# Second MLP product as Strassen's seven half products, queries and keys in a ring of three head groups, output projection's weights fetched per unit

## The chip, the cores and the metric

One core of one Trainium2 chip. The metric is device microseconds of one execution, from the first instruction to the last. The kernel before was run three times: 1659.76, 1660.66 and 1661.33 us, median 1660.66 us.

## The reference, cut to what matters

```python
def A(x, wqkv, wo):                      # x: 2048 x 640, 32 heads of 20
    q, k, v = split(x @ wqkv)            # 640 x 1920
    scores = einsum("hqd,hkd->hqk", q, k) * 20 ** -0.5
    p = softmax(where(0 <= query - key < 256, scores, -1e9))
    return merge_heads(einsum("hqk,hkd->hqd", p, v)) @ wo      # 640 x 640
def B(x, w1, b1, w2, b2):                # w1: 640 x 1536, w2: 1536 x 640
    return relu(x @ w1 + b1) ** 2 @ w2 + b2
for layer in range(2):                   # the same weights in both layers
    x = x + A(layernorm(x), wqkv, wo)
    x = x + B(layernorm(x), w1, b1, w2, b2)
```

Inputs and output are float32.

## The kernel before

**Precision.** Every float32 operand of a dense product is kept as two float16 parts, a high part and the rest, its low part. `mm3` (L256) forms a product as three chains of TensorE matmuls, high by high, high by low and low by high, accumulated in one PSUM tile. Whatever feeds a matmul therefore has two evictions: ScalarE writes the high part, then VectorE the low part (`hh` for the hidden layer at L823 and L826, `qd` for queries and keys at L411 and L414, `od` for the attention output at L733 and L736, `yl` for the layer norm at L348 and L352).

**Units and quads.** The work is cut into 16 units: two layers, each of eight blocks of 256 rows. Since a query sees 256 keys back, a unit needs the keys of its own block and of the block before. The 32 heads are handled as 8 quads of four heads, two quads to a head group. For each quad `max_quad` multiplies queries by keys to find the largest score of each row (matmuls at L523, masked maxima on VectorE at L535), `max_out` transposes the maxima and writes them as two more rows under the queries (L547 to L560), `exp_quad` multiplies again with those rows included and takes the exponential on ScalarE (L585, L598; GpSimd masks at L613 and L617), and `pv_quad` multiplies by the values (L647), copies the result (L659, `ot`) and writes it to DRAM (L664, `o<-ot`). `max_quad` runs three quads ahead of `exp_quad`.

**Through DRAM and back.** Queries and keys are computed for a unit by `stage_qk`, evicted as `qd` (L411, L414), written to DRAM by L445 and L447 (`qk<-qd`) and read back by L451 into `qt` and `kt`, laid out with the head dimension on the partitions. `kt` holds all heads of one block, three of them in turn. The attention output of a unit is read back in `load_o` once all its quads are written: `rs` (L693, the sums of the exponentials, spread over partitions) and `od` (L694). VectorE and ScalarE then make it ready for the output projection in an **od chain** of four pieces on VectorE: reciprocal of `rs` (L726), product (L729), and the low part (L736), with ScalarE's high part (L733) between the last two.

**Layer norm to matmul.** `layernorm` (L273 to L286) leaves its rows with tokens on the partitions. For a unit's queries, keys and values, `ln_cross` (L368 to L371, using `cross`, L335 to L361) makes the high (L348) and low (L352) parts of its two row blocks in `yl`, and four DMA transposes, one for each part of each block (L355), turn them into `yT`. The matmuls of `stage_qk` read `yT`.

**What runs beside what.** In the main loop, unit u carries three kinds of work at once: the quads of unit u (`exp_quad`, `pv_quad`), the `max_quad`s three ahead, and a chain of dense work of other units, sliced in between by `together`. In the steady units the dense chain is, in this order: `stage_qk(u+1)` for the queries, `stage_v(u+1)` (first half), `stage_o(u-1)`, `y_cross(u-1)`, `stage_qk(u+1)` for the keys, the rest of `stage_v`, and `stage_f(u-1)`, which holds the first MLP product (f1, weights `w1`, 180 matmuls of 256 columns), relu on ScalarE (L816), the square on GpSimd (L820), the two evictions into `hh`, a call of `ln_cross(u+2)`, and then the second MLP product (f2): 144 matmuls `acc<-w_s,hh` of 320 columns in four banks, each added to `x` on VectorE (L853) and stored (L862). `load_o(u-1)` is called after the first half quad of unit u. I call the place where f2 of one unit ends and `stage_qk` of the next begins the **unit boundary**.

**What sets the order.** The program is written by a planner that runs while the kernel is built. Each eviction or DMA is a `Job` with an engine, a cost, what it depends on and a priority; `pump` puts out the jobs that it thinks can start, `need` moves its clock to a job's end. What it puts out becomes the order of each engine's queue, and on the chip each engine takes its queue strictly in that order, whenever its turn really comes. All DMAs are issued by SyncE, one queue. There are two PSUM banks for dense tiles, transposes and value products (`mm_tile`), so the matmul after next needs the eviction of the tile two before, and three pairs of banks for scores.

## Time and profile before

| what | before |
|---|---|
| runs | 1659.76, 1660.66, 1661.33 us, median 1660.66 us |
| the profiled execution: its span | 1660.5 us |
| TensorE busy, share of the span | 1595.4 us, 96% |
| VectorE, ScalarE, GpSimd busy | 1032.8, 750.1, 636.8 us |
| TensorE busy between 332 and 1411 us, the steady units | 1077.03 us of 1079.00 |
| moved by DMA | 157.42 MB, mean 95 GB/s |

How to read it: the span of the profiled execution is the time of that one run. The page's first part gives how long each engine was busy, its second part the same in 40 slices of 41.5 us, its fourth the chain of work that ended last. The answers of the trace show groups of instructions as `line engine operation output<-input (partitions x elements, type) xcount`, with the busy time, the mean of one in ns, and the idle time of the engine just before them with its releaser; the timeline shows `start duration engine ...`, in us, with the wait in square brackets; and the windows show, for each stretch, its length and then busy us and count for PE, PEld, DVE, ACT and POOL, the granted TensorE clock, the mean DMA share and GB/s.

### The profile page before, as it was taken

How to read it: one execution, taken by the hardware profiler on the slowest of the kernel's cores; microseconds unless marked ns; L12 is line 12 of the kernel's file. 1: busy time of each engine (PE TensorE's matmuls, PEld its weight loads, DVE VectorE, ACT ScalarE, POOL GpSimd, SP SyncE). 2: the span in 40 equal slices, each digit the busy share in tenths (PEclk: the TensorE clock that was granted, in tenths of full speed). 3: DMA queues.
4: the chain of work that ended last, by engine and by line, in shares of the span. 5: the costliest groups of instructions: out<-in, count | busy, mean ns of one | idle time of the engine just before them, and what ended most of it. 6: DMA issues, size and time to landing. Idle time of an engine off the chain costs nothing.

```text
span 1660.5 us, 44547 instructions
## 1 busy us (share of the span) xinstructions
PE 1595.4 (96%) x17574; PEld 1173.0 (71%) x17574; DVE 1032.8 (62%) x3231; ACT 750.1 (45%) x1616; POOL 636.8 (38%) x1309
## 2 busy tenths in 40 slices
PE   7787899999999999999999999999999999999989
PEld 5564676777777777777777777777777777776667
DVE  7566657675665766566565756657665666757341
ACT  4455534535444454544434354444545444453512
POOL 1343533524344353424414243443534344353512
PEclk9897999999999999999999999999999999999999
DMA  8465214343452534335153433424343352421020
GB/s 245 129 179 155 61 61 107 63 118 84 100 101 60 125 69 113 78 102 118 50 136 74 123 82 104 98 68 118 73 109 80 104 115 50 108 70 53 26 64 17
DMA packets 231484, 157.42 MB, mean 95 GB/s; under 512 B 79468, under 2 KB 215020, under 8 KB 231276
## 3 DMA queue, kind: packets, MB, share of 16 engines
q1 hardware_dynamic: 231276, 154.59, 37.8%
q8 instruction: 138, 2.26, 0.6%
q14 instruction: 70, 0.57, 0.1%
HBM read 84.68 MB, written 52.95 MB: 83 GB/s over the span
## 4 chain that ended last, share of the span: by engine, by line
PE 87%; DVE 5%; ACT 3%; DMA 3%; issue 1%; SPq 1%; POOL 0%; DVEq 0%; ACTq 0%; POOLq 0%
PE acc L256 65%; PE pv L647 10%; PE bb L585 6%; PE bb L523 5%; DVE bb L535 2%; ACT pt L598 2%; DMA qk<-qd 1%; PE tr L547 1%; DMA qk<-yl 0%; DMA w_s<-in_A_wqkv_dram 0%; DVE mx L535 0%; DMA ov<-o 0%; DMA qt<-qk 0%; ACT r L816 0%; SPq L560 0%
## 5 line engine op out<-in xcount | busy, mean ns | idle before, releaser
L535 DVE CUSTOM_DVE_ANT_0 bb<-bb,maskb 128x384 f32<-128x384 f32 (+2 forms) x1024 | 510.4, 565 | 117.3 <-PE bb L523 109.4
L598 ACT ACTIVATE pt<-bb 128x512 f32<-128x512 f32 (+1 forms) x736 | 376.5, 602 | 239.9 <-PE bb L585 239.6
L613 POOL TENSOR_SCALAR_AFFINE_SELECT pt<-pt 128x256 f32<-128x256 f32 x448 | 195.0, 440 | 542.8 <-ACT pt L598 521.4
L256 PE MATMUL acc<-y,w_s 128*128 128x256 f16 x2880 | 331.8, 273 | 4.2 <-DVE y L304 1.4
L256 PE MATMUL acc<-w_s,hh 128*128 128x320 f16 x2304 | 326.2, 299 | 0.0
L256 PEld LDWEIGHTS <-w_s 128*128 128x128 f16 x2880 | 278.5, 98 | 58.2 <-issue 25.7
L256 PE MATMUL acc<-yT,wq_s 128*128 128x256 f16 x2400 | 282.7, 276 | 12.6 <-DVE qd L414 10.6
L256 PEld LDWEIGHTS <-hh 128*128 128x128 f16 x2304 | 221.8, 98 | 97.8 <-issue 15.3
L256 PEld LDWEIGHTS <-wq_s 128*128 128x128 f16 x2400 | 233.7, 99 | 58.0 <-issue 27.8
L617 POOL TENSOR_SCALAR_AFFINE_SELECT pt<-pt 128x256 f32<-128x256 f32 x512 | 217.1, 446 | 64.3 <-ACT pt L598 63.2
L826 DVE TENSOR_TENSOR hh<-r,hh 128x256 f16<-128x256 f32 x192 | 91.7, 499 | 208.4 <-ACT hh L823 200.9
L647 PE MATMUL pv<-pt,vt 128*32 128x128 f32 (+1 forms) x3840 | 188.8, 331 | 2.0 <-POOL pt L617 1.4
L820 POOL TENSOR_TENSOR r<-r 128x256 f32<-128x256 f32 x192 | 113.5, 612 | 184.9 <-ACT r L816 183.4
L659 ACT COPY ot<-pv 128x256 f32<-128x256 f32 x128 | 47.6, 372 | 285.6 <-PE pv L647 285.6
L535 DVE DVE_READ_ACCUMULATOR2_ANT mx<- 128x1 f32 x1024 | 142.7, 139 | 0.1
L256 PE MATMUL acc<-wq_s,yT 128*128 128x320 f16 x960 | 142.0, 301 | 0.1
L647 PEld LDWEIGHTS pv<-pt,vt 128*32 128x32 f32 x3840 | 104.2, 110 | 49.1 <-issue 17.6
L256 PE MATMUL acc<-wo_s,od 128*128 128x320 f16 x900 | 131.9, 301 | 3.6 <-DVE x L758 1.7
L816 ACT ACTIVATE r<-acc,b1s 128x256 f32<-128x256 f32 x192 | 80.6, 471 | 99.8 <-PE acc L256 98.4
L256 PEld LDWEIGHTS <-yT 128*128 128x128 f16 x960 | 93.0, 98 | 40.4 <-issue 7.0
L585 PE MATMUL bb<-qt,kt 62*128 62x128 f16 (+1 forms) x1920 | 109.4, 246 | 10.6 <-DVE mx L535 9.8
L256 PEld LDWEIGHTS <-od 128*128 128x128 f16 x900 | 86.1, 98 | 45.9 <-issue 11.1
(84 smaller groups left out, 1175.7 us busy)
## 6 DMA issues: line engine op xcount, KB each, us to landing
qt<-qk SPq DMA_DIRECT2D x30, 480.0 KB
kt<-qk SPq DMA_DIRECT2D x30, 480.0 KB
qk<-qd SPq DMA_DIRECT2D x17, 640.0 KB
o<-ot SPq DMA_DIRECT2D x256, 42.0 KB
od<-o SPq DMA_DIRECT2D x13, 640.0 KB
qk<-yl SPq DMA_DIRECT2D x13, 640.0 KB
qk<-qd SPq DMA_DIRECT2D x17, 320.0 KB
xt<-in_A_x_dram SPq DMA_DIRECT2D x16, 320.0 KB
```

The lines of the kernel that those rows point to most:

```text
L256: nc.tensor.matmul(acc, lhs(a, c), rhs(b, c), start=(k == 0), stop=(k == 3 * nk - 1))
L523: nc.tensor.matmul(to, qt[r, p, i * P:(i + 1) * P], kt[r, p, a:b], start=True, stop=True)
L535: nc.vector.tensor_tensor_reduce(out=v, in0=v, in1=mask, scale=1.0, scalar=-3.0e38, op0=ALU.add, op1=ALU.max, accum_out=accum)))
L585: nc.tensor.matmul(bb[e][:, k, o:o + w], kt[r, 2 * qd + j, ko:ko + P], qt[r, 2 * qd + j, q0 * P:q0 * P + w], start=True, stop=True)
L598: nc.scalar.activation(box["pt"][:, :o], bb[e][:, k, :o], AF.Exp, scale=SCALE / (QS * QS))
L613: nc.gpsimd.affine_select(out=m, in_=m, pattern=[[0, 2], [-1, P]], compare_op=ALU.is_gt, fill=0.0, base=0, channel_multiplier=1)
L617: nc.gpsimd.affine_select(out=m, in_=m, pattern=[[0, 2], [1, P]], compare_op=ALU.is_ge, fill=0.0, base=0, channel_multiplier=-1)
L647: nc.tensor.matmul(pv[32 * jj:32 * (jj + 1), q0 * P:(q0 + qn) * P], vf[:, c:c + 32], pj[:, j, :], start=(k == 0), stop=(k == len(steps) - ...
L659: nc.scalar.copy(ot[:, qd % 2], pv)
L816: nc.scalar.activation(box["r"], acc[:, f, :], AF.Relu, bias=b1s[:, f0 + f:f0 + f + 1], scale=1.0 / (YS * WS))
L820: nc.gpsimd.tensor_tensor(box["r"], box["r"], box["r"], op=ALU.mult)
L826: nc.vector.tensor_sub(hh[:, 1, f, :], box["r"], hh[:, 0, f, :])
```

## The change

Three things are changed, and a few follow from them.

**f2 in seven half products.** Of the unit's hidden layer (256 rows by 1536) and of w2 (1536 by 640), each is cut in two along both directions. Strassen's scheme forms the four half-size blocks of the result from seven products of sums and differences of blocks, in place of eight. The seven products have 18 matmuls each of 320 columns: 126 a unit in place of 144, 2016 in place of 2304 in all. Each has an accumulator of its own that is added to one or two halves of `x` (L957, 12 adds a unit in place of four). The sums on the hidden side are made for each pair of f tiles, 6 a unit: two relus on ScalarE (L881), two squares and one sum on GpSimd (L885, L892), two sums on VectorE (`mid`, `ends`, L895 and L898), and three high (L907) and three low parts (L910), of 256, 384 and 256 columns. The tiles `ho` and `hw` take the place of `hh`. On the weights' side, seven combinations of w2 are made once at the start for each of 6 k (30 sums on GpSimd, 42 conversions of 320 columns in place of 12 of 640); the sixth k is staged in `r` and `sm`, the tiles in which the first f1 evictions work, and the first relu waits for it.

**A ring of head groups.** `qt` and `kt` give way to three tiles `qg` of queries and three `kg` of keys, each for one head group, with the block before and the unit's own block side by side. Keys are written into one DRAM tile a layer (L473, 3 DMAs) and each group's 256 or 512 keys loaded again for each unit (L503, L508). A matmul of `max_quad` can then run over both blocks: 12 a quad in place of 18, 1504 in place of 2176 in all, over the same columns. The DMAs that load queries and keys go from 72 to 256, and those of the program from 937 to 1162.

**wo from DRAM.** The converted `wo` is written to DRAM once (`wod`) and fetched for each unit with two DMAs right after `rs` and `od` (L753), into the space of `hw`.

With these, `stage_v(u+1, (3,))` and `ln_cross(u+2)` stand between f1 and f2 as chain items of their own, and `add_b2` (GpSimd, L832) is posted with `y_cross`. The instructions of the engines change as follows: PE 29256 to 27336, VectorE 3233 to 3681, ScalarE 1618 to 1736, GpSimd 1311 to 1429 (in the program's own counting).

The core of the diff:

```diff
+    qgs = [sb.tile([P, 4, T], F16, name=f"qg{i}") for i in range(3)]
+    kgs = [sb.tile([P, 4, 2 * T], F16, name=f"kg{i}") for i in range(3)]
-    wo_s = sb.tile([P, 2, KC, D], F16, name="wo_s")
+    wo_s = sb.tile([P, 2, KC, D], F16, name="wo", tag="hw", bufs=1)
+    wod = tc.dram_tile([P, 2, KC, D], F16, name="wod")
-    w2_s = sb.tile([P, 2, FC, D], F16, name="w2_s")
+    w2_s = sb.tile([P, FH, 2, 7, HD], F16, name="w2_s")
+    rt = sb.tile([P, 2, 5, P], F32, name="r")
+    sm = sb.tile([P, HD], F32, name="sm")
...
+        for j, fn, size in ((0, queries, 1.0), (1, keys, 1.6 if g else 1.0)):
+            deps = [w for c0, _, w in wrote[u, j] if c0 <= last]
+            job = dma(fn, int(8 * 3 * DH * T * 2 * size * (1.7 if u > 2 else 1.1)), *deps, n=2, prio=0)
...
+            wos[u] = wt, [dma(lambda wt=wt, a=a: nc.sync.dma_start(wt[:, a], wod[:, a]), P * 2 * KC * D, loaded, *keep,
+                              prio=1) for a in range(2)]
...
+    PRODS = ((1, "w", 2, "s", ((0, 0, 1.0), (0, 1, -1.0))), (4, "w", 3, "s", ((1, 0, -1.0), (1, 1, 1.0))),
+             (2, "o", 1, "o", ((1, 1, 1.0), (0, 1, 1.0))), (3, "w", 0, "d", ((1, 0, 1.0), (0, 0, 1.0))),
+             (0, "o", 2, "o", ((1, 0, 1.0), (0, 1, 1.0))), (5, "o", 0, "o", ((0, 1, 1.0),)),
+             (6, "w", 1, "d", ((1, 0, 1.0),)))
...
+        for t, to, c, k, dests in PRODS:
+            acc, jobs = mm_tile([P, 2 * T], "acc")
...
+            yield from mm3(acc[:, :HD], left, lambda b, f: w2_s[:, f, b, t], FH, 136, then)
...
-            parts += [stage_qk(u + 1, (0,)), stage_v(u + 1, range(2)), stage_o(u - 1), lambda: (y_cross(u - 1), iter(()))[1], stage_qk(u + 1, (1,)), stage_v(u + 1, range(2, 4))]
+            parts += [stage_qk(u + 1, (0,)), stage_v(u + 1, range(2)), stage_o(u - 1), lambda: (y_cross(u - 1), iter(()))[1], stage_qk(u + 1, (1,)), stage_v(u + 1, (2,))]
+            gap = [stage_v(u + 1, (3,))]
             if u + 2 < NU:
-                ahead_ln = u + 2
+                gap.append(lambda u=u: (ln_cross(u + 2, *b2js[u - 1]), iter(()))[1])
...
-        dense = chain(*parts, stage_f(u - 1, ahead_ln))
+        dense = chain(*parts, stage_f1(u - 1), *gap, stage_f2(u - 1))
```

Since the planner lays out the order anew, the queues differ around the unit boundary too. SyncE's queue at one steady unit boundary before: the four transposes of `yl` are the L355 rows, then come the last writes of the attention output (L664) and the loads of `rs` and `od`.

```order
L355 DMA_TRANSPOSE yT<-yl 128x5x128 x2
L862 DMA out_dram<-x_13582 128x640
L355 DMA_TRANSPOSE yT<-yl 128x5x128
L560 DMA qt<-mT 1x8x128 x4
L355 DMA_TRANSPOSE yT<-yl 128x5x128
L664 DMA o_13702<-ot 21x2x256 x4
L693 DMA rs<-o_13702 128x1x256
L694 DMA od<-o_13702 128x5x256
```

The same place after, where the lines are L383, L715, L742 and L743, and L753 is the fetch of `wo`:

```order
L383 DMA_TRANSPOSE yT<-yl 128x5x128 x3
L715 DMA o_15167<-ot 21x2x256 x4
L941 DMA out_dram<-x_15039 128x640
L742 DMA rs<-o_15167 128x1x256
L743 DMA od<-o_15167 128x5x256
L383 DMA_TRANSPOSE yT<-yl 128x5x128
L941 DMA out_dram<-x_15040 128x640
L762 DMA x_16555<-xs_121 128x640
L753 DMA wo<-wod 128x3200 x2
L762 DMA x_16556<-xs_122 128x640
```

The fourth transpose has moved behind the loads of `rs` and `od`, and the loads of `wo` and of `x` stand behind it.

VectorE's queue in the last quad before a steady unit boundary, before: the low parts of the layer norm's two blocks (L352, both at once) stand between one quad's maxima (L535) and an add of f2 (L853).

```order
L535 ISA bb,mx<-bb,maskb 128x3x128
L535 ISA mx 128x1
L853 SCALAR_TENSOR_TENSOR x_15120<-acc,x_15120 128x320
L352 TENSOR_TENSOR yl<-xt,yl 128x640 x2
L552 TENSOR_SCALAR mT<-tr 16x128
```

And after, where the maxima are L583, the low part of the layer norm's second block L380 and the last add of f2 L957:

```order
L583 ISA bb,mx<-bb,maskb 128x3x128
L583 ISA mx 128x1
L583 ISA bb,mx<-bb,maskb 128x3x128
L583 ISA mx 128x1
L380 TENSOR_TENSOR yl<-xt,yl 128x640
L957 SCALAR_TENSOR_TENSOR x_15040<-acc,x_15040 128x320
```

Before, both low parts have another eight maxima of the unit behind them; after, the second one has moved behind the unit's last eight maxima, one instruction ahead of f2's last add.

VectorE's queue across the boundary before, from the last maxima of the unit over the last add of f2 (L853) to the low part of the first two query columns (L414) and the start of the od chain (L726):

```order
L535 ISA bb,mx<-bb,maskb 128x3x128
L535 ISA mx 128x1
L535 ISA bb,mx<-bb,maskb 128x3x128
L535 ISA mx 128x1
L853 SCALAR_TENSOR_TENSOR x_15121<-acc,x_15121 128x320
L414 SCALAR_TENSOR_TENSOR qd<-acc,qd 128x2x256
L726 RECIPROCAL rs<-rs 128x64
```

And after, the twelve rows behind the last add of f2, where the od chain is L780, L783 and L790, and the low part of the query columns L438:

```order
L780 RECIPROCAL rs<-rs 128x64
L783 TENSOR_TENSOR od<-od,rs 128x5x64
L780 RECIPROCAL rs<-rs 128x64
L790 TENSOR_TENSOR od<-od 128x5x64
L783 TENSOR_TENSOR od<-od,rs 128x5x64
L780 RECIPROCAL rs<-rs 128x64
L790 TENSOR_TENSOR od<-od 128x5x64
L783 TENSOR_TENSOR od<-od,rs 128x5x64
L780 RECIPROCAL rs<-rs 128x64
L790 TENSOR_TENSOR od<-od 128x5x64
L783 TENSOR_TENSOR od<-od,rs 128x5x64
L438 SCALAR_TENSOR_TENSOR qd<-acc,qd 128x2x256
```

The query columns' low part has moved from ahead of the od chain to behind its fourth product. Of the twelve steady unit boundaries (those at which units 3 to 14 begin) eleven stand in this order on both engines; at the one where unit 8 begins, the first of the second layer, all four transposes stand ahead of the loads.

On TensorE the order at the boundary is, after: the last value product of the unit (L698, 16 matmuls), 24 matmuls of the last two half products, 16 of `exp_quad` (L634), and then `stage_qk` with 45 matmuls, 12 of `max_quad` (L571), the next value product (L698) and 30 more of `stage_qk`. Before, it is the same with 28 matmuls of f2, 16 of `exp_quad`, 50 of `stage_qk`, 18 of `max_quad` and the value product.

More of the change, by code (lines that the diff above doesn't have):

```diff
@@ L28 @@
 FC = F // P
+FH = FC // 2
 NP = H // 2
@@ new lines, in load_groups, with load_group, of, queries @@
+    def load_groups():
+        while ring["next"] < min(4 * NU, ring["free"] + 3):
+            u, G = divmod(ring["next"], 4)
+            last = (160 * (G + 1) - 1) // P
+            if any(wrote.get((u, j), [(0, 0, None)])[-1][1] <= last for j in range(2)):
+                return
+            load_group(u, G, last)
+            ring["next"] += 1
+    def load_group(u, G, last):
+        l, g = divmod(u, NG)
+        s, ps_ = (4 * u + G) % 3, slice(4 * G, 4 * G + 4)
+        def of(dr, e):
+            return dr.rearrange("(p e d) t n -> e (d t) p n", e=2, d=DH)[e][:, ps_]
+        def queries():
+            for e in range(2):
+                nc.sync.dma_start(qgs[s][64 * e:64 * e + 3 * DH], of(rows_of[u], e))
+        def keys():
+            lo = 0 if g else T
+            for e in range(2):
+                nc.sync.dma_start(kgs[s][64 * e:64 * e + 3 * DH, :, lo:],
+                                  of(kds[l], e)[:, :, (g - 1) * T + lo:(g + 1) * T])
+        for j, fn, size in ((0, queries, 1.0), (1, keys, 1.6 if g else 1.0)):
+            deps = [w for c0, _, w in wrote[u, j] if c0 <= last]
+            job = dma(fn, int(8 * 3 * DH * T * 2 * size * (1.7 if u > 2 else 1.1)), *deps, n=2, prio=0)
+            for q in range(2):
+                trips[u, j, 2 * G + q] = job
+        if u == 0 and G == 2:
+            job.gates.append(gate)
+        if u == 0 and G == 0:
+            job.gates.append(gate0)
```

372 lines of the change are left out of this document (209 added, 163 removed).

## The prediction

> **What bounds the kernel now.** I read the page first, then windows by stage, then the timeline over one unit boundary. The page's span, busy times, the rows of PE and PEclk over 40 slices, and the chain's shares by engine:
>
> ```profile
> span 1660.5 us, 44547 instructions
> PE 1595.4 (96%) x17574; PEld 1173.0 (71%) x17574; DVE 1032.8 (62%) x3231; ACT 750.1 (45%) x1616; POOL 636.8 (38%) x1309
> PE   7787899999999999999999999999999999999989
> PEclk9897999999999999999999999999999999999999
> PE 87%; DVE 5%; ACT 3%; DMA 3%; issue 1%; SPq 1%; POOL 0%; DVEq 0%; ACTq 0%; POOLq 0%
> ```
>
> The windows put the idle time of TensorE in its place (columns: stretch, length, busy of PE, PEld, DVE, ACT, POOL, clock, DMA share, GB/s):
>
> ```profile
> 0.00:332.00 332.00, 286.05 (x2973) 205.64 (x2974) 210.17 (x672) 163.49 (x337) 124.24 (x235) 0.94 0.47 125
> 332.00:1411.00 1079.00, 1077.03 (x12209) 799.67 (x12207) 699.65 (x2195) 489.87 (x1063) 422.45 (x892) 1.00 0.40 94
> 1411.00:1660.50 249.50, 232.30 (x2397) 167.70 (x2395) 122.95 (x365) 96.75 (x216) 90.08 (x182) 0.99 0.21 56
> ```
>
> For 1079 us TensorE is busy for 1077.03 at clock 1.00. Matmuls taken away there are gained in full, and any wait put in there is lost in full. What keeps the unit boundary closed shows in the timeline:
>
> ```profile
> 1005.29 1.55 DVE L352 TENSOR_TENSOR yl<-xt,yl 128x640 f16<-128x640 f32 x2
> 1010.25 1.21 SPq L355 DMA_TRANSPOSE yT<-yl  x1
> 1011.73 0.84 PE L523 MATMUL bb<-kt,qt 60*128 60x128 f16 x18
> 1012.49 1.51 PE L647 MATMUL pv<-pt,vt 128*32 128x256 f32 x32
> 1013.93 3.98 PE L256 MATMUL acc<-w_s,hh 128*128 128x320 f16 x28
> 1014.49 1.36 SPq L664 DMA_DIRECT2D o<-ot  x4
> 1017.19 0.59 SPq L693 DMA_DIRECT2D rs<-o  x1
> 1017.84 0.83 PE L585 MATMUL bb<-qt,kt 62*128 62x256 f16 x16
> 1017.94 0.40 SPq L694 DMA_DIRECT2D od<-o  x1
> 1018.47 0.43 SPq L862 DMA_DIRECT2D out_dram<-x  x1
> 1018.61 5.63 PE L256 MATMUL acc<-yT,wq_s 128*128 128x256 f16 x50
> 1018.95 5.65 SPq L708 DMA_DIRECT2D x<-xs  x2
> 1022.72 0.69 DVE L414 SCALAR_TENSOR_TENSOR qd<-acc,qd 128x512 f16<-128x512 f32 x1 [4.29 <-ACT qd L411]
> 1024.94 1.51 PE L647 MATMUL pv<-pt,vt 128*32 128x256 f32 x32
> 1030.24 0.48 DVE L729 TENSOR_TENSOR od<-od,rs 128x320 f32<-128x320 f32 x1
> ```
>
> f2 ends at 1017.84, `exp_quad` covers 0.77 us, and `stage_qk` starts at 1018.61: its last transpose had been issued at 1010.25, 7.69 us before `od`. VectorE made the low query columns at 1022.72, ahead of the od chain, so the value product at 1024.94 had its bank; the od chain's products ran later, one still at 1030.24, with nobody on TensorE waiting. Both covers are changed.
>
> **The change part by part.**
>
> *f2, less matmuls.* In the timeline of f2, 36 matmuls of 320 columns:
>
> ```profile
> 807.58 5.06 PE L256 MATMUL acc<-w_s,hh 128*128 128x320 f16 x36
> 812.57 0.51 PE L523 MATMUL bb<-kt,qt 60*128 60x128 f16 x10
> ```
>
> (812.57 − 807.58) / 36 = 0.1386 us each. 288 fewer give −39.9 us, all on a bound engine.
>
> *Fewer max matmuls over the same columns.* 18 for a quad take 1012.49 − 1011.73 = 0.76 us. They stream 3072 columns, two at a time on the two halves of the rows; at f2's 320 columns in 0.1386 us that is 1536 columns, 0.665 us. The excess, 0.095 us, can at most go whole: 112 quads are −10.6 us; if columns alone count, 0. I take the third that goes with the count, 0.032 × 112 = −3.5.
>
> *The boundary: a transpose behind `od`.* T is the end of the seventh product. Between the last value product and T stand 24 matmuls, 3.33 us. Before, `od` is issued 1017.94 − 1013.93 = 4.01 us after that product (copy, writes, their landing, `rs`), so after at about T + 0.7. The fourth transpose is now the next on SyncE, T + 1.1, because its low part stands behind eight more maxima on VectorE. How long it takes behind `od` shows in the row of 1018.95: SyncE stood 5.65 us over two loads of `x`, since the second goes into the buffer that the store of 1018.47, issued right behind `od`, reads. That store was thus through at about 1024.2, 5.7 us after its issue. I let the transpose land like it, between T + 6 and T + 7, taking T + 6.4. TensorE has `exp_quad` (0.77 us) and then matmuls that read the low parts from the second on: idle for 5.6 us.
>
> *The boundary: the query columns behind the od chain.* The tail of before has an od chain that was waited for:
>
> ```profile
> 1583.85 0.47 SPq L694 DMA_DIRECT2D ov<-o  x1
> 1590.84 0.89 DVE L729 TENSOR_TENSOR ov<-ov,rs 128x320 f32<-128x320 f32 x2 [0.97 <-DMA ov<-o]
> 1595.59 0.48 DVE L729 TENSOR_TENSOR ov<-ov,rs 128x320 f32<-128x320 f32 x1
> ```
>
> Issue to first use 7.0 us, the four products 1595.59 + 0.48 − 1590.84 = 5.2 us. With landing between 5.5 (a little under the store's 5.7) and 7.0 us, the low query columns (0.69 us, row 1022.72) come at T + 0.7 + 5.5 + 5.2 + 0.7 = T + 12.1 to T + 13.6, and the unit's first value product waits for that bank. Queued behind L438 are the maxima of that quad. TensorE's own work up to there is 0.77 + 45 × 0.1126 (5.63 / 50) + 0.76 = 6.6 us, so this wait alone costs 5.5 to 7.0. It overlaps the first: after T + 6.4 the same matmuls take until T + 12.2 at full clock.
>
> *The clock.* The start of the program shows what a gap does. A wait of 3.51 us, and two windows behind it; a wait of 2.10 us, and one window:
>
> ```profile
> 118.98 1.31 PE L585 MATMUL bb<-qt,kt 62*128 62x256 f16 x8 [3.51 <-DVE mx L535]
> 118.00:121.40 3.40, 2.27 (x14) 1.42 (x14) 3.40 (x7) 2.15 (x5) 1.84 (x2) 0.50 0.00 0
> 121.40:124.70 3.30, 3.30 (x17) 2.13 (x15) 1.88 (x6) 2.18 (x5) 1.99 (x5) 0.50 0.01 1
> 164.98 1.12 PE L256 MATMUL acc<-wo_s,stg 128*128 128x320 f16 x6 [2.10 <-DVE stg L736]
> 165.70:169.10 3.40, 3.40 (x26) 1.83 (x24) 1.86 (x5) 1.50 (x4) 1.31 (x3) 0.50 0.06 23
> ```
>
> The granted clock is 0.50 for 124.70 − 118.98 = 5.7 us in the one case, for 3.4 in the other: half of it is lost, 1.7 to 2.85 us a boundary. The Trainium skill, "TensorE: Matmul & The Clock Gate", section "What's actually happening", has the clock halved after an idle window of about 3.4 us and released after a busy one of the same length. By that alone each boundary loses 1.7 us and a gap under 3.4 us nothing; the gap of 2.10 us here was followed by half clock, so the measurement decides against the second half.
>
> The two waits and the clock together: 5.6 + 1.7 to 2.85 = 7.3 to 8.5 by the transposes, 5.5 to 7.0 by the bank. I take 7.5 us; ends 5.7 (the transpose issued at T + 1.1 with `od`'s shortest landing, with the clock's loss hidden in the second wait) and 9.8 (7.0 + 2.85). Eleven of the twelve boundaries have this order: +82.5 (62.7 to 107.8).
>
> *w2's chain at the start.* TensorE has 46 us of idle time in the first 332, so most of the added loading lies beside it. What is not shown before is the sixth k, whose five sums pass through one buffer, each with a sum on GpSimd and a conversion:
>
> ```profile
> L778 POOL TENSOR_TENSOR x<-x,xt 128x320 f32<-128x320 f32 x60 | 51.0, 878 | 13.2 <-DMA xt<-in_B_b_dram 13.2
> L199 POOL TENSOR_TENSOR w_s<-stg,w_s 128x640 f16<-128x640 f32 x8 | 11.2, 1402 | 19.6 <-ACT stg L198 19.6
> L826 DVE TENSOR_TENSOR hh<-r,hh 128x256 f16<-128x256 f32 x192 | 91.7, 499 | 208.4 <-ACT hh L823 200.9
> L853 DVE SCALAR_TENSOR_TENSOR x<-acc,x 128x320 f32<-128x320 f32 x60 | 29.5, 491 | 82.1 <-PE acc L256 82.1
> ```
>
> Five rounds of 0.88 + 0.7 (half of 1.40) + about 0.5 are 10 us, and the first relu waits for the last. Between nothing and 15; I take 5, as half can be done early.
>
> *Hidden-side sums.* VectorE's f1 work goes from 12 × 0.499 = 6.0 to 6 × (2 × 0.5 + 0.6 + 0.5 + 0.4), 15 us a unit, the adds from 2.0 to 12 × 0.491 = 5.9: +13. Its busy share of 699.65 / 1079 makes 63.8 us of a 98.4 us unit, so 77 of 95: it has room on the mean. In f1's own stretch:
>
> ```profile
> 1063.80:1090.30 26.50, 26.36 (x314) 21.35 (x314) 14.27 (x47) 14.85 (x35) 15.65 (x30) 1.00 0.30 62
> ```
>
> VectorE is 14.27 busy of 26.5, plus 9, 23: still under. Two `r` buffers give a pair 8.8 us for a chain of some 4.5. I take 0; up to 1.2 a unit, 17, if maxima fall in between.
>
> *Loads of the ring and of `wo`.* DMA share is 0.40 in the steady stretch; `wo` is queued behind the transpose and used half a unit later, the ring's loads have most of a quarter unit. Nothing, and beyond that they only lengthen `od`'s landing, which the range holds. The single buffers of `hw` and `hh` free with the last product; `od` went into `hh` before, too.
>
> Sum: 1660.5 − 39.9 − 3.5 + 82.5 + 5 = 1704.6. The median of the runs is 0.16 over the span: 1705.
>
> **The rivals.**
>
> A. The gain shows and the boundary stays closed: the low part and the transposes run far enough ahead, as they did at 1005.29 before, and ScalarE and VectorE get the query columns out. It needs the fourth transpose 5.6 us earlier and the od chain landed early. Against it is the queue itself: SyncE takes it behind `od` and VectorE takes L438 behind the chain, and `od` can't come before the last value product. 1660.5 − 43.4 + 5 = 1622. Chance 0.16, mainly for something in these orders that I misread.
>
> B. Half of it: the transpose, far smaller than `od`, doesn't wait for it. Then 1.21 us of issue and a landing like the writes of 1014.49 (1017.19 − 1015.85 = 1.3) bring it in at T + 3.6, idle 2.8 us; with a chain as much shorter, about 3 us a boundary and no clock loss: 1660.5 − 43.4 + 33 + 5 = 1655. The store behind `od` that took 5.7 us speaks against it. The Trainium skill, "DMA: Bandwidth & Descriptors", section "Queues, rings and completion order", lets each DMA engine consume its descriptors in ring order, with the increment behind all earlier writes; by that rule B's first half cannot be, and the store's row agrees. Chance 0.10.
>
> C. Beyond the forecast, VectorE sets f1's or f2's pace: maxima (8 at 0.5 us) between a pair's sums and its low parts hold the next relu, and the seven accumulators take one of two banks each, with an add behind the same maxima. At 2 us in each of 14 units: 1705 + 28 = 1733. It decides from VectorE over 95% of a stretch; on the count above it is at 23 of 26.5. Chance 0.12.
>
> The main forecast, slower through the boundary, has 0.62; it decides against the gain as soon as a boundary costs more than (39.9 + 3.5 − 5) / 11 = 3.5 us. That seven products are fewer matmuls than eight is fixed by the code, so "it does not do what it says" has no share.
>
> **How the numbers follow.** A single measurement of this kernel can tell about 0.2%, 3.3 us, from no change. Forecast alone: 1660.5 − 50.5 + 62.7 = 1673 to 1660.5 − 39.9 + 107.8 + 15 = 1743. The range reaches from 1640 (B's lower part, at 1.6 us a boundary) to 1742; it leaves out A, 0.16, and 0.04 at the top. Faster: A and half of B, 0.21. Same: 0.03. Slower: 0.76.
>
> **What would show it.** Right: TensorE idle some 5 us at eleven boundaries just behind `exp_quad`, released by a DMA into `yT`; a second wait on `qd` or on the bank before the value product; clock 0.50 in 3 to 6 us after it; a steady unit near 103 us (98.4 − 18 × 0.1386 − 8 × 0.032 + 7.5 = 103.1), not 98.4; and no such gap where unit 8 begins. Wrong: PE busy over 99% between the boundaries and across them (A), or gaps spread over f1 and f2 that VectorE releases (C).

## The result, and the profile after

| | before | after |
|---|---|---|
| median of the runs, us | 1660.25 (4 runs) | 1856.05 (4 runs, 1854.28 to 1857.65) |
| ratio, 95% interval | | 1.1175 [1.1159, 1.119] |
| span of the profiled execution, us | 1660.5 | 1853.0 |

The change costs 11.8%: slower, as forecast, but by 196 us and not by 44, and above the upper end of the range (1742). The page after, in the rows that the prediction showed of before:

```profile
span 1853.0 us, 43882 instructions
PE 1633.3 (88%) x16614; PEld 1151.0 (62%) x16614; DVE 1240.1 (67%) x3679; ACT 793.7 (43%) x1734; POOL 738.0 (40%) x1427
PE   7875699989898998989999898989989899888888
PEclk9986799989999998999999898999999899899999
PE 59%; DVE 15%; POOL 8%; DMA 7%; ACT 5%; issue 5%; SPq 2%; POOLq 0%; DVEq 0%; ACTq 0%
```

TensorE has fewer matmuls and is busy longer: part of them ran at a lower clock, and its share of the chain fell from 87% to 59%. VectorE, GpSimd and DMA took it over. To see where, I cut both spans at the issue of unit 2's load of `rs` (at 338.0 before, 376.5 after) and of unit 13's (1411.1 and 1577.6). Between them lie eleven units. Before, then after, with the columns of the windows shown above:

```profile
0.00:338.00 338.00, 292.05 (x3050) 209.67 (x3051) 214.42 (x688) 163.86 (x338) 124.24 (x235) 0.94 0.46 124
338.00:1411.10 1073.10, 1071.12 (x12133) 795.71 (x12131) 695.41 (x2178) 489.50 (x1062) 422.45 (x892) 1.00 0.40 95
1411.10:1660.50 249.40, 232.20 (x2396) 167.63 (x2394) 122.95 (x365) 96.75 (x216) 90.08 (x182) 0.99 0.21 56
```

```profile
0.00:376.50 376.50, 301.65 (x2920) 208.72 (x2920) 253.69 (x773) 175.11 (x376) 155.78 (x271) 0.90 0.43 125
376.50:1577.60 1201.10, 1098.96 (x11452) 781.61 (x11452) 822.70 (x2464) 514.89 (x1127) 475.80 (x957) 0.96 0.39 108
1577.60:1853.00 275.40, 232.73 (x2242) 160.70 (x2242) 163.74 (x442) 103.68 (x234) 106.47 (x200) 0.96 0.24 70
```

The start is 38.5 us longer, the eleven units 128.0 (11.6 a unit), the tail 26.0. In the units TensorE is now idle for 102 us (1201.1 − 1098.96), where it was 2.

The boundary after, on TensorE, with the end of f2, `exp_quad` and `stage_qk`:

```profile
1241.99 2.61 PE L286 MATMUL acc<-w_s,hw 128*128 128x320 f16 x18
1244.53 0.87 PE L634 MATMUL bb<-qg,kg 62*128 62x256 f16 x16
1245.33 0.28 PE L286 MATMUL acc<-yT,wq_s 128*128 128x256 f16 x1
1252.93 6.57 PE L286 MATMUL acc<-yT,wq_s 128*128 128x256 f16 x44 [7.32 <-DMA yT<-yl]
```

One matmul of `stage_qk` runs, the second waits 7.32 us for a transpose. VectorE and SyncE in the same stretch:

```profile
1244.38 0.82 DVE L380 TENSOR_TENSOR yl<-xt,yl 128x640 f16<-128x640 f32 x1
1245.91 0.59 SPq L742 DMA_DIRECT2D rs<-o  x1
1246.60 0.43 SPq L743 DMA_DIRECT2D od<-o  x1
1247.12 1.23 SPq L383 DMA_TRANSPOSE yT<-yl  x1
1252.40 0.49 DVE L783 TENSOR_TENSOR od<-od,rs 128x320 f32<-128x320 f32 x1 [1.50 <-DMA od<-o]
1256.66 0.49 DVE L783 TENSOR_TENSOR od<-od,rs 128x320 f32<-128x320 f32 x1
1258.58 0.69 DVE L438 SCALAR_TENSOR_TENSOR qd<-acc,qd 128x512 f16<-128x512 f32 x1 [1.43 <-ACT qd L435]
```

The low part was ready at 1245.2, and its transpose stood behind `rs` and `od` until 1247.12. It came in at 1252.9, 0.5 us after `od`. The od chain was through with its fourth product at 1257.15, and L438 then waited for its own high part: this chain delayed nothing. Behind the gap the clock:

```profile
1252.70:1256.10 3.40, 3.17 (x15) 2.25 (x16) 3.28 (x8) 1.25 (x3) 0.00 (x0) 0.50 1.03 421
1256.10:1259.50 3.40, 3.40 (x33) 2.86 (x32) 1.91 (x5) 1.07 (x3) 0.00 (x0) 0.98 0.72 286
```

The granted clock is 0.50 for one stretch of 3.4 us after the matmuls resume, so this gap costs 1.7 us more. Eleven boundaries have such a wait, of 6.4 to 8.5 us; at the one where unit 8 begins it is 0.71 us.

The groups on TensorE over the whole span, before and then after (busy, mean ns, idle time ahead and its releasers), show what else waits:

```profile
L256 PE MATMUL acc<-yT,wq_s 128*128 128x256 f16 x2400 | 282.7, 276 | 12.6 <-DVE qd L414 10.6 <-DVE yT L304 2.1
L647 PE MATMUL pv<-pt,vt 128*32 128x128 f32 (+1 forms) x3840 | 188.8, 331 | 2.0 <-POOL pt L617 1.4 <-POOL pt L613 0.3
L585 PE MATMUL bb<-qt,kt 62*128 62x128 f16 (+1 forms) x1920 | 109.4, 246 | 10.6 <-DVE mx L535 9.8
L523 PE MATMUL bb<-kt,qt 60*128 60x128 f16 (+1 forms) x2176 | 105.1, 236 | 4.5 <-ACT pt L598 4.3
```

```profile
L286 PE MATMUL acc<-yT,wq_s 128*128 128x256 f16 x2400 | 308.6, 290 | 87.6 <-DMA yT<-yl 82.5 <-DVE yT L334 2.6 <-DVE mT L601 0.8
L698 PE MATMUL pv<-pt,vt 128*32 128x128 f32 (+1 forms) x3840 | 213.6, 334 | 9.9 <-POOL pt L665 4.7 <-POOL pt L669 1.9 <-DVE qd L438 0.2
L634 PE MATMUL bb<-qg,kg 62*128 62x128 f16 (+1 forms) x1920 | 117.0, 246 | 30.3 <-DVE mx L583 23.4 <-DMA qg<-mT 6.2
L571 PE MATMUL bb<-kg,qg 60*128 60x128 f16 (+2 forms) x1504 | 110.1, 270 | 31.3 <-ACT pt L650 25.5 <-DMA qg<-mT 5.6
L595 PE MATMUL tr<-ident,mx 128*16 128x128 f32 x64 | 18.1, 283 | 8.7 <-ACT r L881 8.5
```

The boundary is 75.0 us of idle time (87.6 − 12.6) and 25.9 of slower matmuls (308.6 − 282.7), 101 in all. But value products, exp and maxima together have 92 us more (24.8 + 7.6 + 5.0 busy, 7.9 + 19.7 + 26.8 idle), for which the sum had nothing. What releases the maxima is ScalarE's exp, and the value products wait for GpSimd's masks. One quad in f1 after, on TensorE, GpSimd and ScalarE:

```profile
1193.04 0.83 PE L634 MATMUL bb<-qg,kg 62*128 62x256 f16 x16
1193.86 0.83 POOL L892 TENSOR_TENSOR sm<-r 128x256 f32<-128x256 f32 x1
1194.73 0.41 ACT L907 CAST hw<-sm 128x256 f16<-128x256 f32 x1 [1.84 <-POOL sm L892]
1195.04 0.59 ACT L650 ACTIVATE pt<-bb 128x512 f32<-128x512 f32 x1
1196.96 2.55 ACT L650 ACTIVATE pt<-bb 128x512 f32<-128x512 f32 x5
1198.07 0.83 POOL L892 TENSOR_TENSOR sm<-r 128x256 f32<-128x256 f32 x1
1198.87 0.94 POOL L665 TENSOR_SCALAR_AFFINE_SELECT pt<-pt 128x256 f32<-128x256 f32 x2
1200.30 2.67 PE L698 MATMUL pv<-pt,vt 128*32 128x256 f32 x32
1200.67 1.62 POOL L669 TENSOR_SCALAR_AFFINE_SELECT pt<-pt 128x256 f32<-128x256 f32 x3
```

The first exp stands behind a high part that waits 1.84 us for GpSimd's sum, and more high parts stand between the first exp and the other five. Then the next sum (L892 at 1198.07) stands in GpSimd's own queue ahead of the masks, and the value product, which needs them, takes 2.67 us where 32 matmuls took 1.51 before. So there are two places: ScalarE's queue ahead of the exps, and GpSimd's ahead of the masks. Means over ten steady units (3 to 13 without 8), for the first and the second quad in f1, in us from the start of `exp_quad`:

| | last exp ends | last mask ends | value product takes |
|---|---|---|---|
| before | 5.5 and 4.9 | 7.3 and 7.5 | 1.5 and 1.5 |
| after | 6.5 and 7.1 | 9.3 and 9.4 | 2.7 and 2.2 |
| the sums left out (t_noops, below) | 5.5 and 6.3 | 7.2 and 8.2 | 1.5 and 1.8 |

This makes three theories to be tested. For **the boundary**, it is the transpose's place in SyncE's queue. For **f1**, it is the half sums, through these two queues. For **the start**, it is the chain of w2's combinations.

### The profile page after: what moved, and what is told of

The parts are those of the page before. It is cut to its first block, busy times and chain, and to the rows that moved or that the text cites. A ratio compares the mean times of both kernels' runs of the same rounds, so it can differ in the third digit from the quotient of the medians.

```text
span 1853.0 us, 43882 instructions
## 1 busy us (share of the span) xinstructions
PE 1633.3 (88%) x16614; PEld 1151.0 (62%) x16614; DVE 1240.1 (67%) x3679; ACT 793.7 (43%) x1734; POOL 738.0 (40%) x1427
## 4 chain that ended last, share of the span: by engine, by line
PE 59%; DVE 15%; POOL 8%; DMA 7%; ACT 5%; issue 5%; SPq 2%; POOLq 0%; DVEq 0%; ACTq 0%
PE acc L286 43%; PE pv L698 7%; DVE bb L583 5%; PE bb L634 4%; PE bb L571 4%; DMA yT<-yl 4%; POOL r L885 2%; POOL pt L669 2%; ACT pt L650 2%; POOL pt L665 1%; ACT r L881 1%; POOL sm L892 1%; DVE hw L910 1%; DMA o<-ot 1%; DVE r L898 1%
## 5 line engine op out<-in xcount | busy, mean ns | idle before, releaser
L583 DVE CUSTOM_DVE_ANT_0 bb<-bb,maskb 128x384 f32<-128x384 f32 (+2 forms) x1024 | 511.9, 565 | 127.5 <-PE bb L571 121.4
L650 ACT ACTIVATE pt<-bb 128x512 f32<-128x512 f32 x736 | 378.6, 601 | 230.8 <-PE bb L634 230.0
L286 PE MATMUL acc<-yT,wq_s 128*128 128x256 f16 x2400 | 308.6, 290 | 87.6 <-DMA yT<-yl 82.5
L698 PE MATMUL pv<-pt,vt 128*32 128x128 f32 (+1 forms) x3840 | 213.6, 334 | 9.9 <-POOL pt L665 4.7
L885 POOL TENSOR_TENSOR r<-r 128x256 f32<-128x256 f32 x192 | 115.0, 619 | 155.6 <-ACT r L881 131.6
L286 PE MATMUL acc<-w_s,hw 128*128 128x320 f16 x1152 | 171.6, 303 | 4.5 <-ACT hw L907 4.5
L698 PEld LDWEIGHTS pv<-pt,vt 128*32 128x32 f32 x3840 | 107.6, 110 | 96.0 <-POOL pt L669 36.1
L286 PEld LDWEIGHTS <-hw 128*128 128x128 f16 x1152 | 112.1, 99 | 53.7 <-ACT hw L907 5.4
L583 DVE DVE_READ_ACCUMULATOR2_ANT mx<- 128x1 f32 x1024 | 144.7, 141 | 0.0
L634 PE MATMUL bb<-qg,kg 62*128 62x128 f16 (+1 forms) x1920 | 117.0, 246 | 30.3 <-DVE mx L583 23.4
L571 PE MATMUL bb<-kg,qg 60*128 60x128 f16 (+2 forms) x1504 | 110.1, 270 | 31.3 <-ACT pt L650 25.5
L286 PE MATMUL acc<-w_s,ho 128*128 128x320 f16 x864 | 125.6, 299 | 0.0
L634 PEld LDWEIGHTS <-kg 62*128 62x128 f16 x1920 | 74.1, 95 | 72.3 <-issue 59.9
L314 POOL TENSOR_TENSOR bmv<-bmv,neghalf 128x1 f32<-128x1 f32 x64 | 42.8, 669 | 183.1 <-DVE bmv L308 182.9
```

What stands on the lines that cost most here:

```text
L286: nc.tensor.matmul(acc, lhs(a, c), rhs(b, c), start=(k == 0), stop=(k == 3 * nk - 1))
L314: j = post("G", 520, lambda: nc.gpsimd.tensor_tensor(box["mv"][:, 3:4], box["mv"][:, 2:3], neghalf, op=ALU.pow), j, prio=prio)
L571: nc.tensor.matmul(to, qg[r, p, i * P:(i + 1) * P], kg[r, p, z:y], start=True, stop=True)
L583: nc.vector.tensor_tensor_reduce(out=v, in0=v, in1=mask, scale=1.0, scalar=-3.0e38, op0=ALU.add, op1=ALU.max, accum_out=accum)))
L634: nc.tensor.matmul(bb[e][:, k, o:o + w], kg[r, p, kb * P:(kb + 1) * P], qg[r, p, q0 * P:q0 * P + w], start=True, stop=True)
L650: nc.scalar.activation(box["pt"][:, :o], bb[e][:, k, :o], AF.Exp, scale=SCALE / (QS * QS))
```

## The experiments

All spans are of the profiled execution of each kernel; start, units and tail are cut as above. Executions of the kernel before lie between 1656.2 and 1662.7 us, so a difference of less than some 6 us between two single executions proves little.

| kernel | start | eleven units | tail | span |
|---|---|---|---|---|
| before | 338.0 | 1073.1 | 249.4 | 1660.5 |
| after | 376.5 | 1201.1 | 275.4 | 1853.0 |
| t_first: transpose ahead of `od` | 380.3 | 1154.0 | 268.2 | 1802.5 |
| t_early: whole layer norm first | 381.7 | 1170.9 | 267.6 | 1820.2 |
| t_parts: its parts alone earlier | 379.9 | 1124.1 | 268.7 | 1772.7 |
| t_costs: t_parts, other costs | 381.0 | 1120.4 | 266.6 | 1768.0 |
| t_nosums: no half sums | 364.4 | 1156.6 | 254.7 | 1775.7 |
| t_noops: no sums, all parts | 367.4 | 1159.8 | 258.2 | 1785.4 |
| t_w2plain: plain w2 blocks | 349.1 | 1204.9 | 274.8 | 1828.8 |
| t_all: t_parts, t_nosums, t_w2plain | 341.2 | 1084.3 | 246.2 | 1671.7 |
| t_all7: t_all with 7 adds | 341.3 | 1075.6 | 245.3 | 1662.2 |
| t_lowpool: t_all7, low parts on GpSimd | 340.0 | 1069.9 | 243.2 | 1653.1 |
| t_ring: before and the ring | 335.8 | 1072.6 | 249.4 | 1657.8 |
| t_ringwo: and `wo` per unit | 339.4 | 1072.4 | 248.5 | 1660.3 |

**The transpose ahead of `od` (t_first).**

```diff
-        loaded = dma(load, P * (KC + 1) * T * 4, *done, n=2, prio=0)
+        loaded = dma(load, P * (KC + 1) * T * 4, *done, *pre.get(u + 2, ()), n=2, prio=0)
```

> The load of rs and od also waits until the fourth transpose of the next unit's layer norm has been put in the queue, so that SyncE takes the transpose ahead of them; its low part still stands behind the unit's last eight maxima. Theory (the place in the queue behind od): the transpose lands in about 2.7 us as the other three do (2.6 to 2.7 us in the changed kernel, 5.4 to 6.3 behind od), the idle time of 6.9 us a unit in stage_qk falls to 2 to 3.5 us and part of the half clock goes: 4 to 6 us in 11 units, span 1853 to between 1785 and 1810. Rival (the od chain in front of the query columns on VectorE is what ends last): the wait moves to the value product, the span falls by under 15 us.

Measured: span 1802.5, 50.5 us less. The wait for the transpose at one boundary, and the group:

```profile
1215.06 2.20 PE L286 MATMUL acc<-yT,wq_s 128*128 128x256 f16 x14 [2.84 <-DMA yT<-yl]
...
L286 PE MATMUL acc<-yT,wq_s 128*128 128x256 f16 x2400 | 304.9, 287 | 36.9 <-DMA yT<-yl 31.7 <-DVE yT L334 2.6 <-DVE mT L601 0.8
```

The wait for transposes falls from 82.5 to 31.7 us, and no wait takes its place: the place in the queue is the cause, and the rival falls. The half clock stays: behind the gap of 2.84 us it is 0.50 for 3.41 us (1216.09 to 1219.50). The order of the query columns and the od chain changed with this edit too, so that it does not test that order by itself; the trace above already shows that it decided nothing.

**The whole layer norm first (t_early), and its parts alone (t_parts).**

```diff
-        ln_load(u, *deps)
+        ln_load(u, *deps, prio=0)
...
-        pre[u], _ = cross(lns.pop(u), dst, lambda: sb.tile([P, 2, 2, D], F16, name="yl", tag="qd", bufs=1))
+        pre[u], _ = cross(lns.pop(u), dst, lambda: sb.tile([P, 2, 2, D], F16, name="yl", tag="qd", bufs=1), 0)
```

t_parts has only the second of these, with 1 for 0.

> The layer norm for the unit after next and its two parts get the planner's first priority (0 in place of 2), nothing else: the low parts then stand ahead of f2's second maxima, all four transposes ahead of rs and od, and the query columns' low part ahead of the od chain. Theory: the boundary costs nothing again, 9.1 us (6.88 idle, 2.23 of half clock) in 11 units: span 1853 to about 1753 (1745 to 1770). Rival (the wait comes from od's transfer and its chain, which stay): 5 us a boundary are left, about 1800.

> Only the high and low parts and the transposes of the layer norm get priority 1 in place of 2; its sums and its normalization stay where they were. The low part of the second block then stands one place ahead of the unit's last eight maxima, and all four transposes ahead of rs and od. Theory (t_early lost its gain because the whole layer norm stood ahead of eight maxima for which exp waited): neither wait is left, 9 us in 11 units, span 1853 to between 1750 and 1775. Rival (VectorE is so full in f2 that any place of these instructions makes someone wait): exp waits for the maxima again, 2 us and more a unit, 1790 to 1820.

Measured: t_early 1820.2, a miss by 67 us; 1821.0 us median, ratio to before 1.0958 [1.0935, 1.0982]. The boundary is closed (idle ahead of `stage_qk` 5.0 us in all), but exp now waits in f2:

```profile
1215.92 0.27 PE L634 MATMUL bb<-qg,kg 62*128 62x256 f16 x1 [2.97 <-DVE mx L583]
...
L634 PE MATMUL bb<-qg,kg 62*128 62x128 f16 (+1 forms) x1920 | 126.2, 255 | 65.5 <-DVE mx L583 57.7 <-DMA qg<-mT 5.9
```

The layer norm's five kinds of instruction on VectorE stand ahead of eight maxima, exp needs the banks that these free, and 57.7 us are lost there, against 23.4 in the changed kernel. After this gap of 2.97 us the clock is 1.00 for another 0.66 us and then 0.50 for 3.41 us (1216.58 to 1219.99). t_parts puts only the low parts ahead of the unit's last maxima: 1772.7, 1774.07 us median, ratio 1.0682 [1.0664, 1.07], a gain of 80 us where the theory had 99, though inside its range. Exp's idle time is 40.9 us in place of 30.3, so a small part of the rival holds: in f2 both of the places tried for these instructions make exp wait. And at the boundary where unit 8 begins, which had been nearly closed, a transpose is now waited for, 6.72 us.

**Half sums left out (t_nosums), and the sums alone (t_noops).** Both leave out part of the computation. t_nosums, in short (t_noops drops only the three sums):

```diff
-            js = post("G", 571, sums, *sq, *hj["s"][-1:], prio=0)
-            jm = post("D", 210, mid, *sq)
-            je = post("D", 343, ends, js)
-            for k, deps, v, to, c0, n in (("s", [js], s, "w", 2, 2), ("o", [jm, je], r[:, 0:3], "o", 0, 3),
-                                          ("d", [je], r[:, 3:5], "w", 0, 2)):
+            for k, deps, v, to in (("o", sq[:1], r[:, 0:2], "o"), ("d", sq[1:], r[:, 3:5], "w")):
...
-                return ht[to][:, a, f, c]
+                return ht[to][:, a, f, c % 2]
```

> Leaves out the half sums of the hidden layer: the seven products read the squares' high and low parts themselves, so f1's evictions are as many as before the change (12 relu, 12 squares, 12 high and 12 low parts in pairs) while f2 has its 126 matmuls and 12 adds; the boundary keeps its order. Theory (the sums hold exp and the maxima in f1): the 4.8 us a unit in the value products, exp and maxima go, 11 times, and 10 to 25 us at the start and the tail: 1853 to between 1770 and 1795, with the idle time at the boundary as it was. Rival (these waits come from the ring or from the late boundary): under 15 us.

> Leaves out the three sums of each pair alone (one on GpSimd, two on VectorE); the 18 high and 18 low parts a unit stay, and are made from the squares. Theory (exp stands on ScalarE behind high parts that wait for these sums): most of what leaving out sums and parts together gained, 77 us, comes here too: span 1780 to 1800. Rival (it is the number of parts): under 30 us, 1825 and more.

Measured: t_nosums 1775.7, 77.3 us less (units 44.5, tail 20.7, start 12.1); t_noops 1785.4, 67.6 of the 77.3. The groups of t_nosums:

```profile
L698 PE MATMUL pv<-pt,vt 128*32 128x128 f32 (+1 forms) x3840 | 192.9, 332 | 3.3 <-POOL pt L665 2.8 <-DVE qd L438 0.2
L634 PE MATMUL bb<-qg,kg 62*128 62x128 f16 (+1 forms) x1920 | 112.6, 245 | 22.6 <-DVE mx L583 16.3 <-DMA qg<-mT 5.6
L571 PE MATMUL bb<-kg,qg 60*128 60x128 f16 (+2 forms) x1504 | 105.5, 270 | 11.4 <-ACT pt L650 11.1
```

Value products and maxima lose most of their waits, with the boundary as open as before (85.6 us of idle time ahead of `stage_qk`). It is the sums and not the number of parts: six more high and six more low parts a unit are worth the 10 us between the two runs. The runs don't separate ScalarE's queue from GpSimd's; the table above does in part. Without the sums the last mask ends 2.1 and 1.2 us earlier. Of that, 1.0 and 0.8 us are the earlier exps; the rest arises on GpSimd, where its own sum stands ahead of the masks. Exp keeps 22.6 of 30.3 us of idle time. Of the tail's 20.7 us most is again f1 beside quads; the last f2, which follows its f1 with no quad between, waits 3.1 us for its high parts after, 0.2 in t_nosums, and with the clock behind it this is some 5 us.

**Plain blocks of w2 (t_w2plain).** Leaves out the sums of w2's quarters.

```diff
-            for t, x, y, op in ((1, 0, None, None), (4, 3, None, None), (2, 1, 3, ALU.subtract), (3, 2, 0, ALU.subtract),
-                                (0, 0, 3, ALU.add), (5, 0, 1, ALU.add), (6, 2, 3, ALU.add)):
+            for t, x, y, op in ((1, 0, None, None), (4, 3, None, None), (2, 1, None, None), (3, 2, None, None)):
...
-            yield from mm3(acc[:, :HD], left, lambda b, f: w2_s[:, f, b, t], FH, 136, then)
+            yield from mm3(acc[:, :HD], left, lambda b, f: w2_s[:, f, b, t % 4 + 1], FH, 136, then)
```

> Leaves out the sums of w2's quarters: only four plain blocks of 320 columns for each of 6 k are converted (24 conversions, as much data as before the change), and the seven products read those. Theory (the 18 more conversions and 30 sums make the start late): 25 to 35 of the 34 us that the changed kernel loses before unit 2's rs load go, span 1818 to 1828. Rival (the start is late by the half sums of the first f1 or by the ring's loads): under 10 us.

Measured: 1828.8, 24.2 less, just under the 25 to 35 expected; the start 27.4 less, with 3.8 given back in the units. Two waits make up most of it. In the row of L595 above, a transpose of maxima waits 8.5 us for a bank that the first relu must free, and that relu waits for the sixth k; in t_w2plain this is 0.2 us. The larger one is in unit 0's output projection, after and then in t_w2plain:

```profile
L286 PE MATMUL acc<-wo,stg 128*128 128x320 f16 x60 | 14.2, 413 | 19.9 <-ACT stg L787 19.9
L285 PE MATMUL acc<-wo,stg 128*128 128x320 f16 x60 | 10.7, 336 | 5.2 <-ACT stg L786 3.6 <-DVE stg L789 1.6
```

TensorE waits 19.9 us for ScalarE's high parts of the attention output, and 5.2 in t_w2plain. Conversions of w2 stand ahead of these parts in the queues of ScalarE and VectorE, and one of them waits 6.70 us on ScalarE for its sum on GpSimd.

**All three (t_all).** The edits of t_parts, t_nosums and t_w2plain.

> The edits of the parts' priority, of the left-out half sums and of the plain w2 blocks together; leaves out the same parts of the computation as those. Theory (boundary, half sums and w2's chain are all of it): 1853 less about 95, 77 and 27 is 1654, so 1640 to 1670, which is the 40 us of f2 less some 1 us a unit at exp and what the start keeps. Rival (something else in the change, such as the ring's loads or wo's fetch, holds the unit): over 1690.

Measured: 1671.7. The three alone gave 80.3 + 77.3 + 24.2 = 181.8 us, together they give 181.3: they are separate costs. But 1671.7 is over the expected range, and still over the kernel before, though f2 has its 288 matmuls less. So something is left that none of the three explains.

**Fewer adds (t_all7), and the low parts on GpSimd (t_lowpool).** Two looks at the rest; both leave out what t_all does, and five of the twelve adds. The first change is in both, the second in t_lowpool alone; lines left out are marked `...`:

```diff
-    PRODS = ((1, "w", 2, "d", ((0, 0, 1.0), (0, 1, -1.0))), (4, "w", 3, "d", ((1, 0, -1.0), (1, 1, 1.0))),
+    PRODS = ((1, "w", 2, "d", ((0, 0, 1.0),)), (4, "w", 3, "d", ((1, 0, -1.0),)),
...
-                nc.vector.tensor_sub(yl[:, i, 1], y, yl[:, i, 0])
+                    nc.gpsimd.tensor_tensor(yl[:, i, 1], y, yl[:, i, 0], op=ALU.subtract)
```

> As t_all, and five of the twelve adds a unit left out as well: every product is added to one half of x only. Theory (exp still waits in f2 for maxima that stand behind the adds): the idle time ahead of exp, 1.62 us a unit, falls to 0.9 or less and its busy time from 6.61 towards 6.1: 10 to 15 us, span 1657 to 1662. Rival (the adds are beside the point; exp waits for the layer norm's parts): under 5 us.

> As t_all7, and the low parts of ln_cross on GpSimd in place of VectorE. Theory (in f2 the maxima stand behind the second low part, which waits for ScalarE's high part; exp waits for the maxima): of the 1.67 us of idle time ahead of exp the 1.1 in f2 go, and some clock with it: 10 to 15 us, span 1647 to 1652. Rival (exp waits since less TensorE work lies between maxima and exp, whatever VectorE has ahead of them): under 4 us.

Measured: t_all7 1662.2 and t_lowpool 1653.1. Exp's group in t_all7, then in t_lowpool:

```profile
L633 PE MATMUL bb<-qg,kg 62*128 62x128 f16 (+1 forms) x1920 | 114.4, 244 | 33.9 <-DVE mx L582 26.3 <-DVE w_s L197 5.4 <-DVE bst L302 1.5
```

```profile
L636 PE MATMUL bb<-qg,kg 62*128 62x128 f16 (+1 forms) x1920 | 112.9, 245 | 21.4 <-DVE mx L585 14.7 <-DMA qg<-mT 5.3 <-DVE bmv L307 0.7
```

t_all7's total came close to the forecast, for another reason: exp waits as in t_all (34.3 us there), and most of the 9.5 us come from the boundary where unit 8 begins, at which t_all still waited 6.84 us for transposes and t_all7 does not. So the adds are not what holds exp. The low parts are half of what exp waits beyond the kernel before: of 33.9 − 10.6 = 23.3 us of idle time 12.5 go in t_lowpool, and 9.1 of span, a little under the 10 to 15 expected.

**Planner's costs (t_costs).** Nothing is left out.

```diff
-            js = post("G", 571, sums, *sq, *hj["s"][-1:], prio=0)
-            jm = post("D", 210, mid, *sq)
-            je = post("D", 343, ends, js)
+            js = post("G", 830, sums, *sq, *hj["s"][-1:], prio=0)
+            jm = post("D", 450, mid, *sq)
+            je = post("D", 540, ends, js)
```

> The parts' priority of t_parts, and the planner's costs of the half-sum instructions set near the measured durations (GpSimd sum 830 ns in place of 571, VectorE sums 450 and 540 in place of 210 and 343, low parts 550 and 660 in place of 344 and 486). Nothing is left out. Theory (high parts are put ahead of exp on ScalarE because the planner thinks the sums are done): exp, value products and maxima lose 1 to 2.5 us less a unit, span 1773 to between 1735 and 1760. Rival (the engines lack the time wherever the parts stand): 1765 to 1785.

Measured: 1768.0, 4.7 under t_parts. The theory fails: the costs nearer to the measured ones move a few instructions and save little, so the loss in f1 is not mainly a slip of the planner's numbers. ScalarE's high parts wait 54.7 us for GpSimd's sums in place of 88.5, but the value products are busy for 213.2 us in place of 214.6. Less waiting on ScalarE alone thus doesn't free them, which fits the second place, GpSimd's sums ahead of the masks.

**The ring alone (t_ring), and `wo` with it (t_ringwo).** Both have the f2 and w2 of before. t_ring takes over `qgs`, `kgs`, `load_groups` and the 12 matmuls of `max_quad`, t_ringwo also `wod` and L753.

> The kernel before with the ring of three head groups alone: f2, w2 and the resident wo as before. Theory (the ring costs nothing and its fewer matmuls give little): 1655 to 1661, the max matmuls as long as before (5.89 us a unit) within 0.3. Rival (keys loaded twice and three groups of room hold the maxima): idle time ahead of the maxima of 1 us a unit or more, 1672 and more.

> The ring alone, and with it wo written to DRAM once and fetched for each unit behind rs and od, as in the change; f2 and w2 as before. Theory (the fetch is hidden; Strassen's half products bring the whole loss): as the ring alone, 1655 to 1661. Rival (1.6 MB more a unit behind od lengthen od's landing or the loads of the ring): 1665 and more, with idle time at stage_o or the maxima.

Measured: t_ring 1657.56 us median, ratio to before 0.9982 [0.9972, 0.9992]; t_ringwo 1662.51, ratio 1.0015 [1.0006, 1.0025]. The maxima of t_ring:

```profile
L533 PE MATMUL bb<-kg,qg 60*128 60x128 f16 (+2 forms) x1504 | 105.6, 270 | 10.7 <-ACT pt L612 10.3
```

105.6 us busy for 1504 matmuls, 105.1 for 2176 before: here the columns count, not the matmuls. The eleven units are equal (1072.6, 1072.4, 1073.1). So the ring's 2.7 us don't come from the maxima, whose idle time even grew from 4.5 to 10.7 us; most of them are in the start (335.8). With `wo` the start is 3.6 us longer again (339.4), presumably for the first writing of `wo`. By itself, beside the f2 of before, neither part loses time that could explain the 196 us. The ring alone is the one kernel here that computes all and lies under the kernel before, by 0.2%, a difference that its interval only just tells from none.

## Why the prediction was wrong

- **Bound, and f2.** Half right. What makes TensorE wait is lost in full, and the matmuls of f2 cost what the sum says: 36 of them take 5.06 us after (from 1221.69), as before. But "Matmuls taken away there are gained in full" is borne out by no run. In t_lowpool the eleven units take 1069.9 us and before 1073.1, 3.2 less, where 18 matmuls a unit should give 27: TensorE waits at exp and maxima instead.
- **The boundary.** The mechanism was right, in its place and its releaser: a transpose behind `od`, 7.32 us of idle time behind `exp_quad`, clock 0.50 behind it. Sized at 7.5 us a boundary (5.7 to 9.8), it measured 101 us in eleven, 9.2 a boundary, and undoing it gave 80. `od` went out 2.1 us behind f2's end (1246.60 against 1244.5) and not 0.7, so the transpose was in 8.4 us behind that end and not 6.4. The transpose came in 0.5 us behind `od`, which rules out rival B, and the boundary of unit 8 had no such gap, as forecast. The rule of the Trainium skill, "DMA: Bandwidth & Descriptors", section "Queues, rings and completion order", that each DMA engine consumes its descriptors in ring order, agrees: t_first moved the one DMA, and 50.8 us of the waiting went.
- **Query columns behind the od chain.** Wrong as a second wait: `stage_qk` itself was late, and the chain was over at 1257.15 when L438's input came.
- **Hidden-side sums.** This step failed. It put them at 0, up to 17, because VectorE had room on the mean and "two `r` buffers give a pair 8.8 us for a chain of some 4.5". It counted VectorE's busy time and the buffers. The cost is neither: the chain's instructions stand in queues that other work needs. High parts that wait for the sums stand on ScalarE ahead of exps, and GpSimd's sums stand ahead of the masks for which the value products wait. That the sums cost it is shown, 67.6 us by t_noops and 77.3 with the added parts by t_nosums; how much goes by which queue is read from the trace alone. Of the 77.3, 20.7 are in the tail and 12.1 in the start, which the sum did not look at. Rival C named the engine wrongly (VectorE's maxima hold the relu) and had 28 for it.
- **w2's chain.** Sized at 5, 0 to 15; 24.2 measured. "Half can be done early" did not hold: the first relu waited, and behind it a bank. And the term looked only at that relu, while the larger wait lay earlier, at unit 0's output projection, whose parts stand behind w2's conversions on ScalarE and VectorE (14.7 us more than in t_w2plain).
- **Ring and `wo`.** The number came near by luck: −3.5 was forecast and −2.7 measured for the ring, but the forecast had it from shorter maxima, and these took 105.6 us in place of 105.1. The fetch is hidden in the units, as forecast.
- **The clock.** The Trainium skill, "TensorE: Matmul & The Clock Gate", section "What's actually happening", wants an idle window of about 3.4 us ahead of half clock. A gap of 7.32 us was followed by 3.4 us at 0.50, as it says. Gaps of 2.97 us (t_early) and 2.84 us (t_first) were followed by 3.41 us at 0.50, too, so here shorter gaps cost the same 1.7 us, and the measurement decides.

Open: t_lowpool, with the named costs gone, should by the sum be at 1660.5 − 39.9 − 3.5 = 1617; it is at 1653.1. These 36 us, nearly all that f2 was to gain, have no shown cause. Value products, exp and maxima still have 30 us more than before in it (5.0 + 3.5 + 0.7 busy, 1.3 + 10.8 + 8.3 idle); of the 8.3 at the maxima, 6.2 stand in t_ring as well. That the shorter unit leaves VectorE too little time between maxima and exp would fit, but was not tried, nor was the ring left out beside the shorter f2.

## What to carry to other kernels

Work taken off the bound engine is a gain only if what it is traded for fits the queues of the others: ask of each added instruction not how long it is but what stands behind it in its engine's queue while it waits, and who waits for that. When a stage is made shorter, the work that ran beside it has less cover; the sum must look at the places with least cover, the tail, the start and the boundaries, one by one. And when a critical instruction is moved forward, check what it displaces: the same edit was worth 80 us with the parts alone moved and 33 us with the whole layer norm.

## What the runs showed of the hardware

A transpose of 160 KB in f16 that was issued behind a 640 KB load was in 5.8 us after its issue (1247.12 to 1252.93), half a microsecond behind that load; t_first's, ahead of it, was in 3.2 us after its issue (1211.84 to 1215.06). GpSimd took longer for a sum of two regions than for a square in place, and VectorE's short operations spread widely in the changed kernel (min/median/max ns):

```profile
L885 POOL TENSOR_TENSOR r<-r x192: 606/612/922, 211.0 to 1830.8; 128x256 f32<-128x256 f32 x192
L892 POOL TENSOR_TENSOR sm<-r x96: 721/830/923, 212.2 to 1831.5; 128x256 f32<-128x256 f32 x96
L895 DVE TENSOR_TENSOR r<-r x96: 268/293/812, 212.3 to 1831.6; 128x128 f32<-128x128 f32 x96
L898 DVE TENSOR_TENSOR r<-r x96: 401/512/1081, 213.1 to 1832.4; 128x256 f32<-128x256 f32 x96
```

The median of L892 is 830 ns where L885 has 612 for the same size, and L895 takes between 268 and 812 ns.
